# A Fourier layer with two expert networks: the first stage of batch 2 copied by ACT alone, and weights converted later

## The chip, the cores and the metric

One Trainium2 chip, one of its cores. The metric is the device time of one execution in microseconds (us); the median of three runs of the kernel before is 1257.87 us. TensorE (PE) multiplies, VectorE (DVE) and ScalarE (ACT) do element-wise work, GpSimd (POOL) does a little at the start, and DMA queues, most of them fed by SyncE (SP), move data.

## The reference

Input is x with 2 batches of 3008 rows of 256 numbers. Three networks follow one another, all in fp32:

```
X = rfft(x, axis=1);  Yr = Xr @ w_r - Xi @ w_i + b_r;  Yi = Xr @ w_i + Xi @ w_r + b_i
Y = sign(Y) * max(|Y| - 0.01, 0)  (real and imaginary part apart);  y = irfft(Y)
h = y @ w_in;  g = h * clip(h + 3, 0, 6) / 6;  z = g @ w_out                 (256 -> 2048 -> 256)
out = (silu(z @ w_gate) * (z @ w_val)) @ w_out2                              (256 -> 1536 -> 256)
```

## The kernel before, in words

The Fourier transform is done as matmuls in two stages each way, since 3008 = 47 x 64. Products that need more than one pass of PE's fast fp32 format are made of three matmuls (`mm3`): each operand is split into a high part, which ACT copies (`nc.scalar.copy` into fp32r), and a low part, which DVE subtracts (`low`, line 118).

*First stage (P).* `pre(n)` runs for n = 0 to 15, eight for each batch. It loads x for n + 3, multiplies two halves of 512 columns with `fwd1_sb` (line 242), copies both results out of PSUM into one buffer `bs` (line 245 on ACT, line 247 on DVE) and sends that to the scratch tensor `Bd` by a DMA on ACT's queue, one P later. For n above 8 `pre_conv` then makes a step of the weight converter.

*Quads.* The rest of the Fourier layer works on quads: 4 of 24 frequency groups of one batch, 12 quads in all (6 for each batch). The text counts them from 1; the code's p is one less. A quad has these pieces:
- `s2`, here S, two halves (S0, S1): loads z from `Bd` a quad ahead, eight matmuls at line 284, two copies on ACT (lines 288, 289) and one low part on DVE (xl, line 118). A negation of that low part on ACT (line 291) is put off until the next piece of the order begins.
- `ln`, here l, two halves (l0, l1): one converter step, then 24 matmuls (lines 113 to 115), then three DVE operations that add the bias and shrink (yb, yc, yp: lines 319, 321, 323).
- `ia`, here a, two halves: two matmuls (line 330), a copy on ACT, and after the second half a DMA to `Cd`.

The order of all this is the list `seq`, written out by hand. Each engine executes what it is given in that order. For quad p it is l0, a0 of the quad before, a P if some are left, S0 and S1 of the next quad, l1, another P, a1. P 1 to 11 come before quad 1, so two P's stand in quads 1 and 2 and one in quad 3. From quad 9 on (`FROM = 8`) four units of the first network are put into each quad; a unit is one of 16 slices of the 2048 hidden columns for one block of tokens. `post` makes the first block's input (line 416, xah and xal, lines 419 and 118) behind quad 8; `few` then limits PSUM tiles to one ring of five.

*The converter (`conv1`).* The weights come as float64 words. It turns 32 pieces of 128 x 256 into high and low parts of fp32. It is a pipeline: a step at index i makes the low part of piece i - 3 (DVE, line 179), the high part of piece i - 2 (ACT, line 175), the square of piece i + 1 (ACT, line 156), the words of piece i (four DVE operations, lines 164, 165, 166, 172), and issues the load of piece i + 3 on SP (line 151; four buffers). The index starts at -3 and the converter is done after index 34. Steps are made by P's 10 to 16, by every l (24 of them), and by units: before unit n, up to two steps while the index is below 2n + 6.

Behind the quads the units of the first network run for all 12 blocks, with the converter of the second network's weights beside them, and then the second network.

Of the kernel before, what the change touches and what calls it, by code (L numbers as in the profile page):

```python
# [77 lines left out]
def fourier_moe_kernel(ctx: ExitStack, tc: tile.TileContext, x, lin, bias, w1, w2, fwd1, inv2, fwd2,  # L78
# [109 lines left out]
    def pieces(p, name, src, nf, n, into):  # L188
        out = []
        for f in range(nf):  # L190
            t = [p.tile([128, n, 256], F32R, name=f"{name}{i}_{f}") for i in "hl"]
            into[f] = t
            out += [(src[:, f, j], t[0][:, j], t[1][:, j]) for j in range(n)]
        return Convert(out)
# [8 lines left out]
    def ring4(name):  # L203
        return ap_.tile([128, 4 * DIM], F32, tag="bc", name=name, bufs=4)


    NT = NJ // 4
    xt = {}

    def load_x(n):  # L210
        b, i = divmod(n, NT)
        if b < NB:
            xt[n] = xs_p.tile([128, 4 * DIM], F32, tag="xah" if n % 2 else "xal", name=f"x{b}_{i}", bufs=2)
            nc.sync.dma_start(xt[n][:QP], x[b][:, i * 4 * DIM : (i + 1) * 4 * DIM])
# [5 lines left out]
    p = psf[0]([128, 512], "p0")  # L220
    for n in range(3):
        nc.tensor.matmul(p, zeros[:, :128], zeros, start=True, stop=True)
    conv1 = pieces(w1p, "w1", w1, KF1, 2, W1)
# [12 lines left out]
    def pre(n):  # L236
        b, i = divmod(n, NT)
        load_x(n + 3)
        bs = ring4(f"bs{b}_{i}")
        for h in range(2):  # L240
            p = psf[0]([GW, 512], f"p1_{b}_{i}_{h}")
            nc.tensor.matmul(p, fwd1_sb, xt[n][:QP, h * 512 : (h + 1) * 512], start=True, stop=True)
            o = bs[:GW, h * 512 : (h + 1) * 512]
            if h == 0:
                nc.scalar.copy(o, p)
            else:
                nc.vector.tensor_copy(o, p)
        sent()
        out_b.append(lambda: nc.scalar.dma_start(Bd[b][:, i * 4 * DIM : (i + 1) * 4 * DIM], bs[:GW]))
        if i == NT - 1:  # L250
            sent()
# [3 lines left out]
    def sent():  # L255

        for g in out_b:
            g()
        out_b.clear()
# [10 lines left out]
    def load_q(b, Q):  # L270
        if (b, Q) in z_t or Q >= NQ:
            return
        if Q not in m_t:
            m_t[Q] = table("m", fwd2, Q, f"m{Q}", 6)
        z_t[b, Q] = ap_.tile([128, 4, DIM], F32, tag="z", name=f"z{b}_{Q}", bufs=3)
        nc.sync.dma_start(z_t[b, Q], bview[b][:, Q * 4 : Q * 4 + 4, :])

    def s2(b, Q, dh):

        if dh == 0:  # L280
            X[b, Q] = [ap_.tile([128, 2, 4, 3 * K2], F32R, tag=f"x{k}", name=f"x{k}_{b}_{Q}", bufs=2) for k in "hl"]
        p = psf[0]([128, 4, 128], f"p2_{b}_{Q}_{dh}")
        for g in range(4):
            nc.tensor.matmul(p[:, g, :], z_t[b, Q][:, g, dh * 128 : (dh + 1) * 128], m_t[Q][:, g, :],
                             start=True, stop=True)
        hi, lo = (t[:, dh, :, K2:] for t in X[b, Q])
        nhi, nlo = (t[:, dh, :, :K2] for t in X[b, Q])
        nc.scalar.copy(hi, p)
        nc.scalar.mul(nhi, p[:, :, K2:], -1.0)
        low(lo, p, hi)  # L290
        later.append(lambda: nc.scalar.mul(nlo, X[b, Q][1][:, dh, :, 2 * K2 :].bitcast(F32), -1.0))
# [47 lines left out]
    FROM = 8  # L339

    def ahead(p):
        if p < len(ORDER):
            load_q(*ORDER[p])

    def S(p):
        def first():
            ahead(p + 1)
            s2(*ORDER[p], 0)
        return [first, lambda: s2(*ORDER[p], 1)] if p < len(ORDER) else []

    def L(p):
        return [lambda h=h: ln(*ORDER[p], h) for h in range(2)]

    def A(p):
        return [lambda h=h: ia(*ORDER[p], h) for h in range(2)] if p >= 0 else [lambda: None] * 2

    def pre_conv(n):
        pre(n)
        if n > NT:
            conv1.step()  # L360

    P = [lambda n=n: pre_conv(n) for n in range(NB * NT)]
    seq = P[:1] + [prepare] + P[1:NT] + [lambda: load_q(0, 0)] + P[NT : NT + 3] + S(0)
    rest = P[NT + 3 :]
    for p in range(len(ORDER)):
        l, a = L(p), A(p - 1)
        some, rest = rest[:2], rest[2:]
        u = [lambda: unit()] if p >= FROM else []
        seq += [l[0], a[0]] + u + some[:1] + S(p + 1)[:1] + u + S(p + 1)[1:] + [l[1]] + u + some[1:] + [a[1]] + u
        if p == NQ:  # L370
            seq += [lambda: load_ct(blocks[0])]
        if p == FROM - 1:
            seq += [lambda: few.__setitem__(0, True)]
            seq += [lambda: post(blocks[0], 0), lambda: post(blocks[0], 1)]
# [23 lines left out]
    def load_ct(k):  # L398
        ct[k] = xs_p.tile([GW, NP, DIM], F32, tag="ct", name=f"ct{k[0]}", bufs=1)
        p0, p1 = span(k)  # L400
        for b in range(NB):
            j0, j1 = max(p0, b * NJ), min(p1, (b + 1) * NJ)
            if j0 < j1:
                nc.sync.dma_start(ct[k][:, j0 - p0 : j1 - p0, :],
                                  Cd[b][:, (j0 - b * NJ) * DIM : (j1 - b * NJ) * DIM].rearrange("p (j d) -> p j d", d=DIM))

    def post(k, eh):

        if eh == 0:
            xs1[k] = pair(xs_p, "xa")  # L410
        n = ntok(k)
        p0, p1 = span(k)
        p = psf[0]([128, BLK], f"p6_{k[0]}_{eh}")
        for j in range(p0, p1):
            a, z = max(j * QN, k[0]), min((j + 1) * QN, k[1])
            nc.tensor.matmul(p[:, a - k[0] : z - k[0]], ct[k][:, j - p0, eh * 128 : (eh + 1) * 128],  # L416
                             inv2_sb[:, a - j * QN : z - j * QN], start=True, stop=True)
        hi, lo = (t[:, eh, :n] for t in xs1[k])
        nc.scalar.copy(hi, p[:, :n])
        low(lo, p[:, :n], hi)  # L420
# [55 lines left out]
    def unit():  # L476

        n = at[0]
        at[0] += 1

        for _ in range(2):
            if conv1.at < 2 * n + 6 and not conv1.done():
                conv1.step()
        if 0 <= n - 1 < len(units):
            lower(units[n - 1])
        if n < len(units):
            k, f = units[n]
            state[units[n]] = project1(k, f, ntok(k))
        if n >= 2:
            outp(units[n - 2])  # L490
        if n < len(units):
            for step in extra.get(units[n], ()):
                step()
        for f in more:
            f(n)
# [298 lines left out]
```

## Time and profile before

| | |
|---|---|
| median of 3 runs | 1257.87 us (1257.26 to 1258.01) |
| profiled execution | 1256.91 us |
| its span | 1255.1 us |
| mean granted clock of PE | 0.995 |
| busy: PE / DVE / ACT | 1231.8 / 846.3 / 679.9 us |
| chain of work that ended last | PE 90%, DVE 5%, DMA 2%, ACT 2% |

The span runs from the first to the last instruction on the core. Busy time of an engine is the sum of what its instructions took; matmuls are pipelined, so a busy PE is not PE at its peak. In a timeline each row has the start, the duration, engine, line, operation, what is written and read, and in brackets how long the engine sat idle before it and what ended that. In a table of windows each row is a stretch of the span with the busy time of every engine.

### The profile page before, as it was taken

The numbers are of one execution on the slowest core, as the hardware profiler recorded it, in microseconds if no ns is written. First come the engines' busy times: TensorE is split into PE (matmuls) and PEld (weight loads), VectorE is DVE, ScalarE is ACT, GpSimd is POOL, SyncE is SP. The second block draws the span as 40 slices with busy tenths as digits, with TensorE's granted clock in tenths as the row PEclk, the third lists the DMA queues.
The fourth block names the chain that finished last, engine by engine and source line by source line (L and its number), as shares of the span: only waits on it lengthen the run. The fifth ranks groups of instructions, "written<-read, shape, count | busy, mean of one in ns | idle before, by whom it ended". The sixth has DMA issues, their size and how long they took to land.

```text
span 1255.1 us, 15965 instructions
## 1 busy us (share of the span) xinstructions
PE 1231.8 (98%) x5914; PEld 1035.4 (82%) x5914; DVE 846.3 (67%) x1492; ACT 679.9 (54%) x1216; POOL 6.3 (0%) x15
## 2 busy tenths in 40 slices
PE   7889999999999999999999999999999999999998
PEld 2789898788888888888889878888888888888997
DVE  2588768576676676667656567677676676666665
ACT  2354545455555555555555465566556655556554
POOL 1000000000000000000000000000000000000000
PEclk9999999999999999999999999999999999999999
DMA  9974512231321221222132054554544644544551
GB/s 304 275 227 160 160 43 67 90 99 63 102 91 57 93 88 52 85 99 85 52 104 91 31 206 151 201 192 165 209 160 156 234 168 151 214 154 166 204 188 68
DMA packets 50286, 172.85 MB, mean 138 GB/s; under 512 B 4752, under 2 KB 18160, under 8 KB 39456
## 3 DMA queue, kind: packets, MB, share of 16 engines
q1 hardware_dynamic: 41856, 158.55, 36.6%
q10 hardware_dynamic: 8128, 12.58, 2.9%
q8 instruction: 46, 0.75, 0.2%
q0 software_dynamic: 224, 0.69, 0.2%
q14 instruction: 32, 0.26, 0.1%
HBM read 132.75 MB, written 39.06 MB: 137 GB/s over the span
## 4 chain that ended last, share of the span: by engine, by line
PE 90%; DVE 5%; DMA 2%; ACT 2%; issue 1%; ACTq 0%; SPq 0%; DVEq 0%
PE acc L114 12%; PE acc L115 12%; PE acc L113 12%; PE ph L113 7%; PE ph L115 7%; PE ph L114 7%; PE P L652 5%; PE P L654 5%; PE P L653 5%; PE p L416 3%; PE Tb L652 3%; PE Tb L654 3%; PE Tb L653 3%; PE Q L652 1%; PE Q L654 1%; PE Q L653 1%
## 5 line engine op out<-in xcount | busy, mean ns | idle before, releaser
L118 DVE TENSOR_TENSOR gl<-r,gh 128x512 fp32r<-128x512 f32 (+1 forms) x192 | 130.2, 678 | 80.0 <-ACT gh L449 78.8
L430 ACT ACTIVATE r<-ph,three 128x512 f32<-128x512 f32 (+1 forms) x192 | 130.4, 679 | 96.2 <-PE ph L115 77.0
L431 DVE SCALAR_TENSOR_TENSOR r<-r,ph 128x512 f32<-128x512 f32 (+1 forms) x192 | 129.5, 675 | 60.9 <-ACT r L430 60.3
L449 ACT CAST gh<-r 128x512 fp32r<-128x512 f32 (+1 forms) x192 | 117.5, 612 | 87.6 <-DVE r L431 86.7
L113 PE MATMUL ph<-xah,w1l 128*128 128x512 f32 (+1 forms) x384 | 152.1, 396 | 0.7 <-DVE w1l L179 0.7
L113 PE MATMUL acc<-gh,w1l 128*128 128x512 f32 (+1 forms) x384 | 148.3, 386 | 1.2 <-ACT gh L449 1.2
L114 PE MATMUL acc<-gl,w1h 128*128 128x512 f32 (+1 forms) x384 | 148.3, 386 | 0.6 <-DVE gl L118 0.6
L115 PE MATMUL ph<-xah,w1h 128*128 128x512 f32 (+1 forms) x384 | 148.2, 386 | 0.0
L114 PE MATMUL ph<-xal,w1h 128*128 128x512 f32 (+1 forms) x384 | 148.2, 386 | 0.0
L115 PE MATMUL acc<-gh,w1h 128*128 128x512 f32 (+1 forms) x384 | 148.1, 386 | 0.0
L118 DVE TENSOR_TENSOR gl<-s,gh 128x512 fp32r<-128x512 f32 (+1 forms) x144 | 97.3, 676 | 49.0 <-ACT gh L676 48.8
L652 PE MATMUL P<-xo,slot 128*128 128x512 f32 (+1 forms) x288 | 111.2, 386 | 1.5 <-DVE g L722 0.8
L114 PE MATMUL acc<-gl,slot 128*128 128x512 f32 (+1 forms) x288 | 111.1, 386 | 0.5 <-DVE gl L118 0.5
L113 PE MATMUL acc<-gh,slot 128*128 128x512 f32 (+1 forms) x288 | 111.1, 386 | 0.5 <-ACT gh L676 0.5
L653 PE MATMUL P<-xo,slot 128*128 128x512 f32 (+1 forms) x288 | 110.9, 385 | 0.0
L654 PE MATMUL P<-xo,slot 128*128 128x512 f32 (+1 forms) x288 | 110.9, 385 | 0.0
L115 PE MATMUL acc<-gh,slot 128*128 128x512 f32 (+1 forms) x288 | 110.9, 385 | 0.0
L718 ACT ACTIVATE s<-g 128x512 f32<-128x512 f32 (+1 forms) x72 | 44.8, 623 | 93.1 <-DVE g L716 93.1
L676 ACT CAST gh<-s 128x512 fp32r<-128x512 f32 (+1 forms) x144 | 88.2, 612 | 0.9 <-DVE s L732 0.6
L114 PEld LDWEIGHTS acc<-gl,w1h 128*128 128x128 f32 x384 | 72.1, 188 | 15.3 <-DVE gl L118 1.7
L113 PEld LDWEIGHTS acc<-gh,w1l 128*128 128x128 f32 x384 | 72.1, 188 | 15.2 <-ACT gh L449 1.6
L113 PEld LDWEIGHTS ph<-xah,w1l 128*128 128x128 f32 x384 | 72.2, 188 | 14.1 <-issue 0.8
(95 smaller groups left out, 2291.4 us busy)
## 6 DMA issues: line engine op xcount, KB each, us to landing
slot<-Wd SPq DMA_DIRECT2D x72, 1152.0 KB, 5.0
st<-in_w SPq DMA_DIRECT2D x68, 256.0 KB, 3.2
Wd<-slot SPq DMA_DIRECT2D x12, 1152.0 KB, 4.7
x<-in_x SPq DMA_DIRECT2D x16, 384.0 KB, 6.5
Bd<-bs ACTq DMA_DIRECT2D x16, 384.0 KB, 4.9
z<-Bd SPq DMA_DIRECT2D x12, 512.0 KB, 5.5
Cd<-cs ACTq DMA_DIRECT2D x12, 512.0 KB, 3.4
Xd<-x SPq DMA_DIRECT2D x20, 256.0 KB, 2.1
```

The lines of the kernel that those rows point to most:

```text
L113: nc.tensor.matmul(o, wl, xh, start=start, stop=False)
L114: nc.tensor.matmul(o, wh, xl, start=False, stop=False)
L115: nc.tensor.matmul(o, wh, xh, start=False, stop=stop)
L118: nc.vector.tensor_tensor(out=o, in0=full, in1=hi.bitcast(F32), op=ALU.subtract)
L430: nc.scalar.activation(r[:, :n], p[:, :n], AF.Relu, bias=three)
L431: nc.vector.scalar_tensor_tensor(out=r[:, :n], in0=r[:, :n], scalar=6.0, in1=p[:, :n], op0=ALU.min, op1=ALU.mult)
L449: nc.scalar.copy(hi[:, :n], g[:, :n])
L652: nc.tensor.matmul(o, wl, x[:, 0, :n], start=start, stop=False, skip_group_check=not start)
L653: nc.tensor.matmul(o, wh, x[:, 1, :n], start=False, stop=False, skip_group_check=not start)
L654: nc.tensor.matmul(o, wh, x[:, 0, :n], start=False, stop=True, skip_group_check=not start)
L676: nc.scalar.copy(hi[:, :nb], t[:, :nb])
L718: nc.scalar.activation(s0[:, :n], h, AF.Silu)
```

## The change

The copy of the second half of a P goes to ACT in batch 2 (eight copies). The converter steps of P's 10 to 16 are gone (seven). One step is added behind each of quads 3 to 8 (six), as the last piece of the quad; behind quad 8 it stands ahead of `post`.

```
             o = bs[:GW, h * 512 : (h + 1) * 512]
-            if h == 0:
+            if h == 0 or b:
                 nc.scalar.copy(o, p)
             else:
                 nc.vector.tensor_copy(o, p)
...
     def pre_conv(n):
         pre(n)
-        if n > NT:
-            conv1.step()
...
         seq += [l[0], a[0]] + u + some[:1] + S(p + 1)[:1] + u + S(p + 1)[1:] + [l[1]] + u + some[1:] + [a[1]] + u
+        if 2 <= p < FROM:
+            seq += [lambda: conv1.step()]
         if p == NQ:
             seq += [lambda: load_ct(blocks[0])]
```

## Rows read from the trace of the kernel before

**Rows 1.** The page's head and busy time by engine.
```profile
span 1255.1 us, 15965 instructions
...
PE 1231.8 (98%) x5914; PEld 1035.4 (82%) x5914; DVE 846.3 (67%) x1492; ACT 679.9 (54%) x1216; POOL 6.3 (0%) x15
```
**Rows 2.** Windows: quad 3, quad 4, quad 7; busy by engine, PE clock, DMA.
```profile
62.40:73.70 11.30, 11.30 (x78) 9.76 (x76) 10.62 (x24) 4.59 (x12) 0.00 (x0) 1.00 0.71 220
73.70:88.20 14.50, 10.93 (x73) 10.36 (x73) 11.43 (x26) 7.60 (x19) 0.00 (x0) 0.88 0.78 259
...
108.20:118.20 10.00, 9.60 (x72) 9.15 (x72) 8.34 (x19) 4.90 (x12) 0.00 (x0) 1.00 0.48 160
```
**Rows 3.** Timeline of PE: S of quad 4, and quad 4's l0.
```profile
68.16 1.95 PE L284 MATMUL p<-m,z 128*128 128x128 f32 x16
...
76.56 0.39 PE L113 MATMUL p<-linh,xl 128*128 128x256 f32 x1 [2.70 <-DVE xl L118]
...
78.49 0.58 PE L113 MATMUL p<-linh,xl 128*128 128x256 f32 x1 [0.87 <-DVE xl L118]
```
**Rows 4.** Timeline of DVE: quad 4's second xl, then one period, quad 6 to 7.
```profile
77.74 0.69 DVE L118 TENSOR_TENSOR xl<-p,xh 128x512 fp32r<-128x512 f32 x1 [1.24 <-ACT xh L289]
...
105.87 0.68 DVE L118 TENSOR_TENSOR xl<-p,xh 128x512 fp32r<-128x512 f32 x1
107.80 0.69 DVE L118 TENSOR_TENSOR xl<-p,xh 128x512 fp32r<-128x512 f32 x1 [1.24 <-ACT xh L289]
108.41 0.41 DVE L179 TENSOR_TENSOR w1l<-wt,w1h 128x256 fp32r<-128x256 f32 x1
...
112.11 0.42 DVE L179 TENSOR_TENSOR w1l<-wt,w1h 128x256 fp32r<-128x256 f32 x1
...
114.10 0.69 DVE L319 TENSOR_TENSOR yb<-p,bias_sb 128x512 f32<-128x512 f32 x1
...
115.89 0.68 DVE L118 TENSOR_TENSOR xl<-p,xh 128x512 fp32r<-128x512 f32 x1
```
**Rows 5.** Timeline of ACT between the two xl.
```profile
106.59 0.42 ACT L291 ACTIVATE xl<-xl 128x256 fp32r<-128x256 f32 x1 [2.89 <-DVE xl L118]
```
**Rows 6.** The chain, in order of time: start, length, work (one matmul of l; one a).
```profile
95.15 0.12 PE p L113
...
96.95 0.87 PE p L330 x4
```
**Rows 7.** Line 247: min/median/max ns, first and last start.
```profile
L247 DVE COPY bs<-p x16: 679/686/689, 8.5 to 73.2; 96x512 f32<-96x512 f32 x16
```
**Rows 8.** Timelines of DVE and PE: the first block's input and its first reader.
```profile
132.15 1.28 DVE L118 TENSOR_TENSOR xal<-p,xah 128x512 fp32r<-128x512 f32 x2
...
134.36 0.39 PE L114 MATMUL ph<-xal,w1h 128*128 128x512 f32 x1
```
**Rows 9.** Timelines of SP and PE: a z, a wait, and the S that reads z.
```profile
110.43 0.39 SPq L276 DMA_DIRECT2D z<-Bd  x1
...
118.57 0.39 PE L113 MATMUL p<-linh,xl 128*128 128x256 f32 x1 [0.42 <-DVE xl L118]
...
121.77 0.50 PE L284 MATMUL p<-m,z 128*128 128x128 f32 x3
```
**Rows 10.** The tile z: time of its DMAs from issue to landing.
```profile
DMA to landing us min/median/max: 3.7/5.5/8.9
```
**Rows 11.** Timelines of DVE and PE, the second stretch without room.
```profile
188.25 0.69 DVE L431 SCALAR_TENSOR_TENSOR r<-r,ph 128x512 f32<-128x512 f32 x1 [0.24 <-ACT r L430]
...
198.23 0.47 PE L113 MATMUL ph<-xah,w1l 128*128 128x512 f32 x1 [0.42 <-DVE w1l L179]
...
210.53 0.69 DVE L118 TENSOR_TENSOR gl<-r,gh 128x512 fp32r<-128x512 f32 x1 [0.50 <-ACT gh L449]
```
**Rows 12.** Windows around the one fall of the clock.
```profile
74.60:78.00 3.40, 1.07 (x6) 0.83 (x6) 2.02 (x5) 2.35 (x7) 0.00 (x0) 1.00 0.99 333
78.00:81.40 3.40, 2.91 (x13) 2.91 (x14) 3.26 (x8) 2.28 (x6) 0.00 (x0) 0.50 0.39 107
```

More of the change, by code (lines that the diff above doesn't have):

```diff
@@ L243, in pre @@
             o = bs[:GW, h * 512 : (h + 1) * 512]
-            if h == 0:
+            if h == 0 or b:
                 nc.scalar.copy(o, p)
@@ L358, in pre_conv @@
         pre(n)
-        if n > NT:
-            conv1.step()
     P = [lambda n=n: pre_conv(n) for n in range(NB * NT)]
@@ L369, in fourier_moe_kernel @@
         seq += [l[0], a[0]] + u + some[:1] + S(p + 1)[:1] + u + S(p + 1)[1:] + [l[1]] + u + some[1:] + [a[1]] + u
+        if 2 <= p < FROM:
+            seq += [lambda: conv1.step()]
         if p == NQ:
```

## The prediction

> **What bounds the kernel now.** I read the page's head first: PE is busy for 1231.8 us of a span of 1255.1 us [rows 1], so a change on ACT and DVE can cost or give only where PE waits for one of them. Then I cut the stretch that the change touches into windows of one quad each. Quads run l0, a0, (P), S0, (P), S1, l1, (P), a1 on PE, where l is the projection, S the next quad's spectrum and a the inverse stage. In quad 3 PE is busy for the whole 11.30 us [rows 2], as it is in quad 2: with the P steps of batch 2 inside them, PE itself sets their length. In the next window PE is busy for 10.93 of 14.50 us. The timeline of PE shows where: quad 4's l0 waits 2.70 us and then 0.87 us for the DVE line that writes xl, the low part of S [rows 3].
>
> From quad 4 on the timeline of DVE repeats itself every 10.02 us (105.87 to 115.89) [rows 4]. Its only idle time is 1.24 us, between the two xl of a quad, and ACT explains it: ACT's negation of the first xl waits for DVE, and the copies that the second xl reads are queued behind it [rows 5]. Everything else in the period is back to back: xl, xl, step, the three operations behind l1, step, the three behind l0. PE needs about 9.4 us for such a quad: 48 matmuls at 0.12 us and two a's at 0.87 us [rows 6], and an S pair at 1.95 us [rows 3]. So quads 4 to 8 are paced by the DVE string, by little (10.02 against 9.4), although the window shows PE at 9.60 and DVE at only 8.34 of 10.00 us [rows 2].
>
> **Part 1, what leaves quads 1 to 3.** Five DVE copies of 0.686 us [rows 7] leave, and seven conversion steps, of which two lie ahead of quad 1. This frees DVE, but PE already ran those quads without waiting, so they get no shorter. The gain is the wait that follows them. S of quad 4 begins on PE at 68.16 and its two halves take 1.95 us [rows 3]. The first half is there at 69.1; ACT then needs about 0.9 us for its two copies (in the loop the second xl starts 1.21 us behind ACT's negation of 0.42 us at 106.59, and the two copies lie between [rows 4, 5]), and may still hold the second copy of the last P and two DMA issues, which I put at 0 to 0.3 us. So the first xl starts at 70.0 to 70.3, and the second, 1.93 us later by the loop (105.87 to 107.80) [rows 4], at about 72.2. Before, it started at 77.74 [rows 4]: DVE is 5.5 us ahead there, and l0 of quad 4 needn't wait.
>
> ACT's eight extra copies I cost at nothing: they lie in quads where PE is the bound, and ACT drops seven steps' work there. If ACT were full, a copy would cost up to what DVE's took, 0.686 us, and as it releases a bank and a DMA sooner the other end is as much below nothing; I take 0, since five of them in series before S still left the xl on time above.
>
> **Part 2, the six steps that come back.** A step takes DVE 1.99 us, from the low part at 112.11 to the next operation at 114.10; after an xl it is 1.92 us [rows 4]; I take 1.95. Each stands at the end of a quad, ahead of the next l0, so on DVE it stands between two full strings, and not in the 1.24 us hole, which is between the two xl. A quad then takes DVE 10.02 + 1.95 = 11.97 us against PE's 9.4. DVE cannot run ahead either: its next xl needs S of the same quad. What ends late is thus the xl of each quad, and PE's l0 behind it.
>
> The sum goes along the DVE string, from quad 4's second xl to the first xal that the first block of the network needs. Before, that is 77.74 [rows 4] to about 132.75 (the first of two that begin at 132.15 and together take 1.28) [rows 8]: 55.0 us. After, it is 55.0 + 6 x 1.95, less 0.4 because l1 of quad 3 has no low part yet (its row is 0.41 [rows 4]): 66.3 us. From 72.2 that gives 138.5. PE read it at 134.36 [rows 8], so the first block starts some 4.2 us later (3.9 to 4.3, by where in 72.0 to 72.3 the second xl falls). Behind that point the units of the first network fill PE, and the loss stays what it is.
>
> The loads go with the steps. Each step issues one on SP (z's own issue there is 0.39 us [rows 9]), which waits until DVE has read the buffer four pieces back; behind it in SP's queue are the tables and z of a quad two ahead. In the trace such a z went out at 110.43 and S of quad 9 began at 121.77, 11.3 us later [rows 9], for a landing of 5.5 us (median) [rows 10]. The added step before it puts z back by one step and one group behind l (3.7 us, 108.41 to 112.11 [rows 4]), while S moves with the longer quad: some 4 us of cover stay. I take 0; without that cover it is up to 3.7 us. Two loads also leave the time before quad 1, where z of quad 1 is on its way: between 0 and two issues, 0.8 us, less; z goes out before them, so I take 0.
>
> On ACT each step has a square and a high part, both behind DVE work that is at least one group old; the copies of S behind them are due later than DVE can take them. 0.
>
> **Part 3, the seventh step.** Seven leave and six return, so from quad 9 on the converter is one step behind, until unit 10, whose own rule (at least 2n + 6) then runs one step that it did not run before. That falls on about 187 us, at the head of the second stretch without room on DVE: after a gap of 0.24 us at 188.25 it has no wait on another engine until 0.50 us at 210.53, and PE waits inside it, 0.42 us for a w1l at 198.23 [rows 11]. A step put ahead of this is passed on less the gap: 1.95 - 0.24 = 1.7 us. Its bounds are 0 (all hidden) and 1.99; I take 1.7, as PE is already waiting.
>
> **Sum.** +4.2 + 1.7 = +5.9 us. The profiled execution took 1256.91 us (span 1255.1 [rows 1], 1.8 us around it), so it would be 1262.8. It lies 0.96 us below the median of the runs, 1257.87; on that median the forecast is 1263.8.
>
> **The clock.** From 78.0 to 81.4 the granted clock was 0.50 (1.2 GHz), after a stretch with 1.07 us of PE work in 3.40 us [rows 12]. It cost nothing on DVE's string, so losing it gains nothing beyond the above. Afterwards PE will wait about 2.6 us in each of quads 4 to 8 and about 3 us ahead of the first block.
>
> **Rivals.**
> - *PE's clock falls at the wait ahead of the first block.* For it: that wait is as long as the one of 2.70 us [rows 3] that the fall followed. Against: in the loop before, waits such as the 0.42 us at 118.57 [rows 9] brought none. 3.4 us at half speed cost 1.7 us where PE is the bound: +7.6 us, 1265.5. Falls inside quads 4 to 8 hide in PE's 2.6 us.
> - *The second tight stretch swallows the late step.* For it: PE's waits there are short. Then +4.2 us, 1262.1.
> - *DVE's extra steps are covered (the other side: faster).* Its place is quads 4 to 8: if the steps fitted into PE's 10.0 us, only the 5.5 us ahead would count. By busy time 8.34 + 1.7 just fits into 10.04. PE gains the waits of 2.70 and 0.87 and some 1.1 us at the low clock (half of 18 matmuls at 0.12 us), 4.7, and loses 1.7: -3.0, 1254.9. It decides if the 1.24 us hole, and the 0.4 us of gaps between DVE's instructions, take up the step. Against: the hole opens and closes with ACT's negation [rows 5], which the step doesn't stand next to.
> - *It evens out.* Half of the steps are covered and the gain pays for the rest: 1257 to 1259. For it: the DVE work is the same but for the copies, and only its place changes.
>
> A rule of the Trainium skill speaks for the third: "Perfetto Trace Analysis", section "Identifying the Most-Contended Engine", finds the bottleneck by the highest occupancy, and for TensorE by its weight loads. In quad 7 that is PE (weight loads 9.15 of 10.00 us, DVE 8.34 [rows 2]), and DVE would have room. The row of 1.24 us that comes back in every quad is why I believe the chain and not the occupancy.
>
> **How the numbers follow.** Forecast (+5.9) 0.60; clock 0.13; late step swallowed 0.13; evens out 0.08; covered 0.06. The range takes in the first three with their bounds: 1262.1 less 2 for what z, the start and the order of ACT may differ, 1260.0; 1265.5 plus 2 for a late z, 1267.5. A measurement of this kernel tells 0.2%, 2.5 us, from no change. Faster by more: 0.06, the covered case. Within: 0.09, the one that evens out and an edge of the swallowed one. Slower: 0.85.
>
> **What would show it.** In the trace of the changed kernel: l0 of quad 4 starts at about 73.7 without a wait; the xl of quads 5 to 9 come every 12.0 us, with the 1.24 us before the second as before; the first ph starts around 138; DVE busy share is low in quads 1 to 3; the wait for w1l near 202 grows from 0.42 to about 2. I am wrong if the period of quads 4 to 8 stays near 10, if PE waits in quads 1 to 3 for ACT's copies, or if S waits for a z.

## The result and the profile after

The changed kernel takes 1266.04 us (median of 4 runs, 1263.85 to 1267.95) against 1257.94 for the kernel before; the ratio is 1.0069, 95% interval 1.0057 to 1.0081. Two later comparisons on other chips gave 1.0045 (1.0032 to 1.0058; 1264.71 against 1258.71) and 1.0052 (1.0039 to 1.0065; 1264.36 against 1258.10). It is slower by 6 to 8 us, clear of the 2.5 us that can be told from no change.

The page of the profile after, head and busy time by engine (that execution took 1266.66 us), against [rows 1]:

```profile
span 1264.9 us, 15963 instructions
...
PE 1237.3 (98%) x5914; PEld 1040.1 (82%) x5914; DVE 841.3 (67%) x1484; ACT 684.2 (54%) x1224; POOL 6.3 (0%) x15
```

DVE has 5.0 us less to do and PE 9.8 us more span. Windows of the profile after: quad 3, quad 4, a quad's length further on, and then three stretches around the first block's input (busy time by engine, PE clock, DMA share, GB/s), against [rows 2]:

```profile
62.40:73.70 11.30, 11.30 (x80) 9.99 (x78) 5.66 (x12) 5.00 (x11) 0.00 (x0) 1.00 0.84 265
73.70:85.00 11.30, 10.53 (x79) 9.70 (x78) 9.47 (x23) 5.43 (x14) 0.00 (x0) 1.00 0.69 210
97.00:109.00 12.00, 9.98 (x72) 9.14 (x72) 10.17 (x24) 5.41 (x14) 0.00 (x0) 1.00 0.56 177
129.40:132.80 3.40, 1.33 (x9) 0.90 (x8) 2.09 (x5) 1.18 (x3) 0.00 (x0) 1.00 0.99 302
132.80:136.20 3.40, 3.40 (x20) 3.40 (x20) 3.26 (x8) 2.26 (x7) 0.00 (x0) 0.56 0.45 149
136.20:139.60 3.40, 3.40 (x18) 3.40 (x18) 3.19 (x8) 1.79 (x4) 0.00 (x0) 0.50 0.69 223
```

In quad 3 DVE falls from 10.62 to 5.66 us, and PE still needs all of the 11.30. From quad 5 on a quad lasts 12.0 us. Ahead of the first block's input PE is busy for only 1.33 of 3.40 us, and nearly all of the next 6.8 us runs at half clock.

The timeline of DVE after: quad 4's second xl, one period, and the first block's first low part, against [rows 4, 8]:

```profile
73.08 0.69 DVE L118 TENSOR_TENSOR xl<-p,xh 128x512 fp32r<-128x512 f32 x1 [1.24 <-ACT xh L289]
...
94.82 0.68 DVE L118 TENSOR_TENSOR xl<-p,xh 128x512 fp32r<-128x512 f32 x1
96.75 0.69 DVE L118 TENSOR_TENSOR xl<-p,xh 128x512 fp32r<-128x512 f32 x1 [1.24 <-ACT xh L289]
...
106.82 0.68 DVE L118 TENSOR_TENSOR xl<-p,xh 128x512 fp32r<-128x512 f32 x1
...
139.05 0.68 DVE L118 TENSOR_TENSOR xal<-p,xah 128x512 fp32r<-128x512 f32 x1
```

The period is 12.00 us (94.82 to 106.82), with the same hole of 1.24 us. The timeline of PE after: l0 of quad 4, a later l0, the first block's input, its first reader, and the late wait for a w1l, against [rows 3, 8, 11]:

```profile
73.55 0.47 PE L113 MATMUL p<-linh,xl 128*128 128x256 f32 x1
...
95.56 0.39 PE L113 MATMUL p<-linh,xl 128*128 128x256 f32 x1 [1.16 <-DVE xl L118]
97.49 0.38 PE L113 MATMUL p<-linh,xl 128*128 128x256 f32 x1 [0.86 <-DVE xl L118]
...
132.47 0.32 PE L416 MATMUL p<-inv_sb,ct 96*128 96x94 f32 x1 [2.07 <-ACT xh L288]
...
142.33 0.39 PE L114 MATMUL ph<-xal,w1h 128*128 128x512 f32 x1
...
207.76 0.50 PE L113 MATMUL ph<-xah,w1l 128*128 128x512 f32 x1 [1.81 <-DVE w1l L179]
```

The wait at quad 4 is gone; in its place l0 of quads 5 to 8 waits, 0.86 to 2.02 us each. The first block's reader (the first matmul that reads xal) moved by 7.97 us, from 134.36 to 142.33; behind it the two profiled executions differ by 1.83 us more (9.80 in span).

The wait of 2.07 us at 132.47 is put down to an ACT copy for quad 9's S1 that ended at 132.43 (0.57 us from 131.86); ahead of it on ACT stands the negation of quad 9's first xl, before which ACT had waited 2.70 us for DVE. The tile ct came late as well: SP issued its load at 127.59, after a wait for a store of cs to Cd, where before it was issued at 122.99, and it landed 4.7 us later, at 132.3. In three other profiles of the moved steps the same wait stands with ct named (2.20, 2.30 and 1.82 us), so which of the two ends it differs between executions.

**Where the 9.8 us of this pair of executions went.** DVE had the first xal ready at 139.7, 6.9 us later than before; PE had 1.6 us of slack there, so the string alone moves the reader by about 5.3 us. PE reads it 2.6 us later still: the clock was at 0.50 (1.2 GHz) from 133.2 to 140.1, over the first block's input and l0 of quad 9. The rest, 1.8 us, is the late step. From the first block's reader to the end of the span it is 1120.7 us before and 1122.6 after; in the eight other profiles below with six steps in place of seven it is 1122.5 to 1123.4, but 1120.5 in the one where the seventh step is put back. The fall of the clock at about 208 us in this execution is not the cause: three of the eight have no fall there and show 1122.5 to 1123.0.

### The profile page after: what moved, and what is told of

Its sections match the earlier page's. It is cut to its first block, busy times and chain, and to the rows that moved or that the text cites. A ratio compares the mean times of both kernels' runs of the same rounds, so it can differ in the third digit from the quotient of the medians.

```text
span 1264.9 us, 15963 instructions
## 1 busy us (share of the span) xinstructions
PE 1237.3 (98%) x5914; PEld 1040.1 (82%) x5914; DVE 841.3 (67%) x1484; ACT 684.2 (54%) x1224; POOL 6.3 (0%) x15
## 4 chain that ended last, share of the span: by engine, by line
PE 91%; DVE 5%; DMA 2%; ACT 1%; issue 1%; SPq 0%; DVEq 0%; ACTq 0%
PE acc L114 12%; PE acc L115 12%; PE acc L113 12%; PE ph L113 7%; PE ph L115 7%; PE ph L114 7%; PE P L652 5%; PE P L653 5%; PE P L654 5%; PE p L416 3%; PE Tb L653 3%; PE Tb L652 3%; PE Tb L654 3%; PE p L242 1%; PE Q L653 1%; PE Q L652 1%
```

## The experiments

Twelve runs were made, in three groups of four; those of a group share a chip and the runs of the kernel before. The changed kernel stands in two of the groups, and two other kernels in two groups each.

**Each part alone.** First the copies:

```
-            if h == 0:
+            if h == 0 or b:
```

> The first part alone: batch 2's first stage is copied by ACT alone, the converter steps stay where they were before. Theory (the DVE string sets quads 4 to 8): five copies of 0.61 to 0.69 us leave DVE's string, so the second xl of quad 4 comes near 74.6 instead of 77.74, the period of quads 4 to 8 stays 10.02 us, the first block's second matmul is at about 131.3, and the time falls by about 3 us to 1254.9. Rival (ACT's copies cost something, or PE is the bound in quads 4 to 8): no change, 1258, or slower.

Measured: 1255.65 us against 1257.72, ratio 0.9982 (0.9973 to 0.9991). DVE in that run, the first xl of all, quad 4's second, and a period further on:

```profile
38.36 0.69 DVE L118 TENSOR_TENSOR xl<-p,xh 128x512 fp32r<-128x512 f32 x1 [15.80 <-ACT xh L289]
...
76.41 0.69 DVE L118 TENSOR_TENSOR xl<-p,xh 128x512 fp32r<-128x512 f32 x1 [1.24 <-ACT xh L289]
...
96.44 0.69 DVE L118 TENSOR_TENSOR xl<-p,xh 128x512 fp32r<-128x512 f32 x1 [1.24 <-ACT xh L289]
...
106.46 0.69 DVE L118 TENSOR_TENSOR xl<-p,xh 128x512 fp32r<-128x512 f32 x1 [1.24 <-ACT xh L289]
```

The period is the old one, 10.02 us, and the gain is 2 us of the 3 expected; the interval leaves out 1, but 2 us is less than the 2.5 that can be told. Quad 4's second xl came at 76.41 and not near 74.6. The copies are not what fell short: the first xl of this execution was 1.65 us late, and from there to quad 4 DVE's string gained 2.98 us, the worth of five copies. The same first xl in the kernel before:

```profile
36.71 0.69 DVE L118 TENSOR_TENSOR xl<-p,xh 128x512 fp32r<-128x512 f32 x1 [8.26 <-ACT xh L289]
```

The 1.33 us that is left at quad 4 is still there at the first xal (130.81 against 132.15), and the reader moved by 1.20, from 134.36 to 133.16: the string carries the gain through. This execution (1257.18 us) is the second slowest of eleven: behind the reader it is 1.5 us longer than the kernel before, with a fall of the clock from 227.4 to 230.9. Why its start was late was not tried.

Then the steps, with the copies left on DVE:

```
     def pre_conv(n):
         pre(n)
-        if n > NT:
-            conv1.step()
...
+        if 2 <= p < FROM:
+            seq += [lambda: conv1.step()]
```

> The second part alone: the converter steps are moved as in the change, but batch 2's second halves are copied by DVE as before. Theory: DVE has room in quads 1 to 3 once the steps are gone, so the copies are worth nothing there and the time is that of the change, 1266 (within 1.5). Where the 0.9 us came from by which quad 4's xl were later than forecast is seen here too: if from the ACT copies, quad 4's second xl is at about 72.2 and not at 73.08. Rival (ACT copies carry part of the result): 1268 to 1269.

Measured: 1265.93 us, ratio 1.0063 (1.0050 to 1.0075), the loss of the whole change: it is in the steps. Quad 4's second xl stood at 72.43; whether that comes from the copies is taken up below.

**The place of a step.** The six steps stand between S0 and S1 of the same quads:

```
-        seq += [l[0], a[0]] + u + some[:1] + S(p + 1)[:1] + u + S(p + 1)[1:] + [l[1]] + u + some[1:] + [a[1]] + u
-        if 2 <= p < FROM:
-            seq += [lambda: conv1.step()]
+        mid = [lambda: conv1.step()] if 2 <= p < FROM else []
+        seq += [l[0], a[0]] + u + some[:1] + S(p + 1)[:1] + u + mid + S(p + 1)[1:] + [l[1]] + u + some[1:] + [a[1]] + u
```

> The change, but the six steps stand between S0 and S1 of the same quads, beside DVE's wait of 1.24 us, and not at the end of the quad. Theory: a step of 1.95 us then costs DVE only what it is longer than the wait; with ACT's two more operations ahead of S1's copies the period of quads 4 to 8 is 10.7 to 11.0 us instead of 12.0, the first block starts 6 to 7 us earlier than in the change, the clock doesn't fall there, and the time is about 1258.5. Rival (the number of steps on DVE counts, not the place): period 12.0, 1266.

Measured: 1257.28 us, ratio 1.0000 (0.9991 to 1.0009), 8.7 us below the steps alone on the same chip. DVE in that run, over one quad:

```profile
90.99 0.68 DVE L118 TENSOR_TENSOR xl<-p,xh 128x512 fp32r<-128x512 f32 x1
91.59 0.41 DVE L179 TENSOR_TENSOR w1l<-wt,w1h 128x256 fp32r<-128x256 f32 x1
...
93.55 0.69 DVE L118 TENSOR_TENSOR xl<-p,xh 128x512 fp32r<-128x512 f32 x1
...
101.64 0.68 DVE L118 TENSOR_TENSOR xl<-p,xh 128x512 fp32r<-128x512 f32 x1
```

The hole is gone: the step lies between the two xl, and the period is 10.65 us instead of 12.00 with the same work. The wait was DVE's only slack, and of the two places tried only this one uses it. The reader came at 131.75, 2.6 us earlier than in the kernel before, and the late step takes 1.9 of that back. The steps alone differ from this kernel by the copies too; the changed kernel, which differs by the place alone, ran on other chips.

**The clock at the first block.** The change with PE kept busy ahead of the first block's input:

```
+    def warm():
+        pw = acc_bank([128, 512], "pw")
+        for _ in range(2):
+            nc.tensor.matmul(pw, zeros[:, :128], zeros, start=True, stop=True)
...
+        if p == FROM - 1:
+            seq += [warm]
```

> The change with two matmuls of zeros more (about 0.86 us each) on PE behind quad 8, where PE waits about 2.1 us ahead of the first block's input. Theory (the fall of the clock from 133 to 140 us costs the part that the DVE string doesn't explain): the granted clock is 1.0 there, the first block's second matmul moves from 142.3 to about 139.7, the time falls by some 2.6 us to 1263.4. Rival (the fall is covered, DVE's string alone sets the first block): the first block starts at 142.3 as before, 1266.

Measured: 1265.57 us, ratio 1.0059 (1.0046 to 1.0071). The clock stayed up over that stretch and the first block's reader came at 140.55, 0.1 us behind its data instead of 2.6; the time showed hardly any of it beside the steps alone (0.4 us), and the changed kernel was not in this group. Since that left the price of the fall open, the last group repeated it as a square: copies on ACT or DVE, with and without the zeros.

> The changed kernel as the corner of a square of four on one chip: copies of batch 2's second halves on ACT or on DVE, with or without the two matmuls of zeros ahead of the first block's input. Theory: 6 to 8 us above the kernel before; a fall of the clock of 6.8 us over the first block's input in most executions.

> The change with the two matmuls of zeros. Theory (the fall ahead of the first block costs up to 2.6 us in the executions in which it happens): 1.5 to 2.6 us below the change on the same chip. Rival (what is saved there is lost again later, or the zeros' own 1.7 us delay what follows): within 0.7 us of the change, as the first pair of chips suggested.

> Steps moved, copies on DVE as before, with the two matmuls of zeros. Theory: quad 4's second xl comes 0.7 to 1.3 us earlier than with ACT's copies, which wait for a buffer of Bd; with the clock held that reaches the first block, and this corner is the fastest of the four, 2 us or more below the steps alone. Rival (the wait for ct sets the first block): no better than the change with zeros.

> Steps moved, copies on DVE as before, no zeros: the fourth corner. Theory: within 1 us of the change on the same chip, at or below it; the copies on ACT are worth nothing once the steps are gone from quads 1 to 3. Rival (the copies help the change): 1 us or more above it.

| | no zeros | zeros |
|---|---|---|
| copies on ACT (the change) | 1264.36 (1.0052, 1.0039 to 1.0065) | 1264.84 (1.0052, 1.0040 to 1.0064) |
| copies on DVE | 1266.38 (1.0066, 1.0054 to 1.0078) | 1264.42 (1.0054, 1.0041 to 1.0067) |

The profile of the changed kernel in this group caught an execution of 1263.45 us in which the clock did not fall there. Timeline of DVE and of PE, and windows:

```profile
71.96 0.69 DVE L118 TENSOR_TENSOR xl<-p,xh 128x512 fp32r<-128x512 f32 x1 [1.24 <-ACT xh L289]
...
131.31 0.32 PE L416 MATMUL p<-inv_sb,ct 96*128 96x94 f32 x1 [0.52 <-ACT xh L288]
...
138.67 0.50 PE L114 MATMUL ph<-xal,w1h 128*128 128x512 f32 x1 [0.48 <-DVE xal L118]
...
204.62 0.50 PE L113 MATMUL ph<-xah,w1l 128*128 128x512 f32 x1 [1.83 <-DVE w1l L179]
```
```profile
128.50:131.90 3.40, 2.88 (x21) 2.46 (x21) 2.09 (x5) 1.18 (x3) 0.00 (x0) 1.00 1.01 325
131.90:135.30 3.40, 3.40 (x32) 3.40 (x32) 3.26 (x8) 2.48 (x7) 0.00 (x0) 1.00 0.46 123
135.30:138.70 3.40, 2.92 (x22) 2.43 (x20) 3.19 (x9) 1.71 (x5) 0.00 (x0) 1.00 0.69 226
```

PE is busy for 2.88 us where it had 1.33, the clock stays at 1.00, and the reader waits for DVE's xal at 138.67: here the string alone sets it. It is the same program, 3.2 us faster than the execution above; 1.1 us of that was there at quad 4's second xl (71.96 against 73.08). With copies on DVE the fall is there in the profile without zeros and not in the one with them. Windows of both, first without, then with:

```profile
135.20:138.60 3.40, 3.40 (x18) 3.40 (x18) 3.16 (x8) 1.89 (x5) 0.00 (x0) 0.50 0.80 229
```
```profile
135.20:138.60 3.40, 3.40 (x29) 3.32 (x27) 3.16 (x8) 2.00 (x5) 0.00 (x0) 1.00 0.77 219
```

That pair differs by 2.0 us in the median, with intervals that overlap, and its readers stand at 141.67 and 139.58 though the data were ready at 139.4 and 139.5. In the five profiles with the fall the reader comes 2.3 to 2.8 us behind its data, in the four of the moved steps without it 0.1 to 0.3 us. So the fall costs some 2 to 2.7 us at the reader in an execution that has it. The traces show that much; in the medians it is not clear of the noise. With copies on ACT the zeros gained nothing: the kernel without them escaped the fall in its profile anyway. With them the first block's input began at 133.09 instead of 131.31, behind the zeros (from 131.37), but the reader stood only 0.3 us behind its data (139.74). Zeros are no sure cure.

The guess that ACT's copies delay quad 4's xl is true in part. In the profile after, and in that of the slow execution of the change below, an ACT copy of the last P waited 1.5 to 1.6 us for a store of bs to Bd, and the second xl of quad 4 came 13.6 to 13.7 us behind that of quad 3. In the four other profiles with the copies on ACT and the steps at the ends of the quads that wait is 0.55 to 0.77 us and the distance 12.8 to 12.9; with the copies on DVE ACT has no such wait at the last P, and the distance is 12.9 in all three. ACT in the profile after, and in the one of 1263.45 us:

```profile
68.80 0.58 ACT L245 COPY bs<-p 96x512 f32<-96x512 f32 x1 [1.53 <-DMA Bd<-bs]
```
```profile
67.67 0.58 ACT L245 COPY bs<-p 96x512 f32<-96x512 f32 x1 [0.77 <-DMA Bd<-bs]
```

Whether the copies help once the steps are moved is not settled: 2.0 us for them here, with intervals that overlap, nothing in the first group, and the rows differ by the fall.

**The seventh step.** The change again, and with one step more behind quad 9:

```
-        if 2 <= p < FROM:
+        if 2 <= p <= FROM:
```

> The changed kernel itself, timed beside the others on one chip: 1265 to 1267, with a scatter of some 4 us between executions that goes with the granted clock (theory: PE now waits in many places, and where the clock falls differs from one execution to the next). Rival (the scatter was chance): runs within 1.5 us of each other, as the run with the steps moved alone had them.

> The change with the seventh step put back, behind quad 9, ahead of the stretch from 190 to 220 us, in which DVE has no room. Theory: DVE has gaps in quads 9 and 10, the step costs nothing there, unit 10 no longer runs one of its own, and PE's wait of 1.81 us for a w1l at 207.8 falls back to about 0.4; the time falls by 1.7 to 2.0 us, against the change on the same chip. Rival (DVE is so late behind quad 8 that a step there is passed on as well): no change.

Measured: 1264.71 and 1263.01 us, 1.7 us apart, with ratios of 1.0045 (1.0032 to 1.0058) and 1.0039 (1.0025 to 1.0053) that overlap; the row is clearer than the times. PE in the second:

```profile
205.44 0.47 PE L113 MATMUL ph<-xah,w1l 128*128 128x512 f32 x1 [0.41 <-DVE w1l L179]
```

The wait is back at its old size, 0.41 instead of 1.81 us. The scatter was there too: 1263.92 to 1269.37 us for the change, 1260.99 to 1269.86 with the seventh step. The slowest run of the change, the profiled one, had the low clock of the start until 44.2 us instead of 37.7 and its second xl of quad 4 at 75.48; the other four lie within 1.1 us.

**A version that beats both.** The copies on ACT, the steps of the P's where they were, and in quads 1 to 8 l1's step moved between S0 and S1:

```
-        if not conv1.done():
+        if not conv1.done() and (h == 0 or ORDER.index((b, Q)) >= FROM):
             conv1.step()
...
-        seq += [l[0], a[0]] + u + some[:1] + S(p + 1)[:1] + u + S(p + 1)[1:] + [l[1]] + u + some[1:] + [a[1]] + u
+        mid = [lambda: conv1.step()] if p < FROM else []
+        seq += [l[0], a[0]] + u + some[:1] + S(p + 1)[:1] + u + mid + S(p + 1)[1:] + [l[1]] + u + some[1:] + [a[1]] + u
```

> The copies on ACT alone, the converter's steps at the P's as before, and in quads 1 to 8 the step of l1 moved between S0 and S1, beside DVE's wait of 1.24 us. Theory: DVE's string of a quad falls from 10.02 to about 8.7 us, below PE's 9.4, so quads 4 to 8 are paced by PE, no xl is waited for, and the first block's second matmul comes at 127.5 to 129 instead of 134.36: 1251 to 1252.5. Rival (the inverse stage's way through memory, from Cd to ct, sets the first block once DVE doesn't): PE waits for ct ahead of the first block's input and the gain stops at about that of the copies alone, 1255.

and then with one step more behind quads 9, 10 and 11:

```
+        if FROM <= p < FROM + 3:
+            seq += [lambda: conv1.step()]
```

> The run before, with one step more behind each of quads 9 to 11, where DVE has gaps. Theory: the units then have three steps less to make in the stretch without room, PE's three waits there (together 1.3 us with what follows them) go, and the time is about 1.2 us below the run before. Rival (steps in quads 9 to 11 are not free): equal or slower.

Measured: 1249.66 us, ratio 0.9932 (0.9920 to 0.9944), and 1247.50 us, ratio 0.9909 (0.9896 to 0.9922), against 1258.71. The first gains more than was expected (its reader came at 126.94); the second is 2.2 us below the first, where 1.2 was expected, with intervals that touch. Who PE waited for between quad 3 and the end of the second tight stretch (us in total, times, longest), in the changed kernel and in the first of the two:

```profile
PE p L113 <- DVE xl L118: 6.2, 7, 1.2
PE p L416 <- ACT xh L288: 2.1, 1, 2.1
PE ph L113 <- DVE w1l L179: 1.8, 1, 1.8
```
```profile
PE ph L113 <- DVE w1l L179: 0.7, 2, 0.4
PE acc L114 <- DVE gl L118: 0.3, 1, 0.3
```

In the second the list is empty. DVE in it, one period, and a window of 9.40 us, for [rows 4, 2]:

```profile
97.15 0.69 DVE L118 TENSOR_TENSOR xl<-p,xh 128x512 fp32r<-128x512 f32 x1 [0.53 <-ACT xh L289]
...
106.41 0.69 DVE L118 TENSOR_TENSOR xl<-p,xh 128x512 fp32r<-128x512 f32 x1 [0.53 <-ACT xh L289]
```
```profile
92.50:101.90 9.40, 9.40 (x76) 9.18 (x75) 8.53 (x19) 5.01 (x12) 0.00 (x0) 1.00 0.55 174
```

A quad takes 9.26 us (97.15 to 106.41), DVE waits in it, and PE is busy throughout: now PE sets it. The wait for ct did not take over.

## Why the prediction was right

1263.8 us was forecast, in a range of 1260.0 to 1267.5; the medians on three chips are 1264.4 to 1266.0. The profiled execution was forecast at 1262.8 and took 1266.66; nearly all of the 3.9 us between lies ahead of the first block's reader: 0.9 at quad 4, 0.35 in DVE's string (66.65 us against 66.3), 2.6 by the clock. The steps:

- *Quads 1 to 3 get no shorter, and quad 4's wait goes:* right. l0 of quad 4 began at 73.55 without a wait. The second xl, forecast at 72.2, stood at 73.08 in the profile after, 71.96 in the later one, and 75.48 in the execution with the long low clock at the start. The forecast gave ACT 0 to 0.3 us for what it may still hold; its copies also wait for a store of bs to Bd, up to 1.6 us, which the forecast left out.
- *A quad takes 11.97 us:* 12.00 (a step costs 1.98 us, against 1.95). PE's own need is 9.26, against the 9.4 taken. This is the term that decides, and moving the same step up to between S0 and S1 took 1.35 us off each quad.
- *The first block's reader at 138.5:* 138.67, waiting for DVE, in the execution in which the clock stayed up; 142.33 in the one where it fell.
- *The late step, 1.7 us:* the wait for w1l grew from 0.42 to 1.81 us and went back to 0.41 with the step returned; behind the reader it costs 1.8 us in this pair, and 1.7 in the medians.
- *Falls of the clock inside quads 4 to 8 hide:* right. In the profile after it was low from 109.3 to 112.7, and the next xl kept the period.
- *The clock at the first block,* a rival at 0.13 for +1.7 us: its size was too small, and its chance too low. The fall is in five of the six profiles with steps at the ends of the quads and without zeros (the change three times, the seventh step, the steps alone twice), lasts 6.8 us and not 3.4, and keeps the reader 2.3 to 2.8 us behind its data. An execution without it, on another chip, took 6.5 us more than the profiled one before, near the sum of +5.9. The +8.1 of the first comparison lies inside the range because the range took in this rival; the comparisons on the other two chips gave +6.0 and +6.3, and how often the fall came in the runs without a profile isn't known. What was missed is that PE stands idle in front of the first block's input and not behind it: I had the input early and PE waiting for xal, but ct, whose load goes out 4.6 us later than before, and ACT's copy for quad 9, itself late behind DVE's first xl, hold it back. In the five profiles with the fall PE waits 1.8 to 2.3 us there, in the sixth 0.52.
- *Covered, or evened out:* neither. The place between the xl covers a step; the end of a quad does not. By the rule of the Trainium skill on occupancy ("Perfetto Trace Analysis", "Identifying the Most-Contended Engine") PE would set quads 4 to 8. The trace differs: with DVE's string longer PE waited, and with it shorter the quad fell from 10.02 to 9.26 us. Occupancy hid a wait of 1.24 us that belongs to DVE's string.

## What to carry to other kernels

An engine that is 83% busy can still be the bound, if its idle time is one wait inside its own chain: add the wait to its work before calling it slack, and put movable work inside that wait. Work that is moved from a stretch where it lies beside a busier engine to one where its engine sets the pace costs its full length each time, however little the total changes. Before moving a step, list for each stretch of the schedule which engine ends last there, and by how much.

## What the runs showed of the hardware

The granted clock falls at different places in executions of the same program. The changed kernel ran once with low clock at 109, 133 to 140 and 208 us (1266.66 us) and once at 97 and 121 us, where DVE's string hides it (1263.45 us). Behind the low clock at 121 PE came to the last a before the first block's input 10.13 us after quad 8's second xl instead of 8.62 (at 129.76 and 129.37); it waited for the input 0.52 us instead of 2.07, and the clock stayed up. That the earlier fall kept the later one away fits these two profiles, but no run tests it.

The longer runs of the change are those with a low mean clock: of its fifteen runs the four at 0.991 or below took 1266.66 to 1269.37 us, the eleven at 0.992 or above 1263.45 to 1265.41. The scatter doesn't follow from the number of PE's waits: the steps alone, with as many of them as the change, spread over 0.65 us in one group and 4.3 in another. All profiles have a low clock at the start, some 7 us long (about 30 to 37 us in the kernel before, beside the fall of [rows 12]); in two it lasted longer, some 14 and 10 us, and why was not tried.
